# Sharing the last weight matrix 13 to 15 between the lower and upper 64 partitions, with its odd blocks on another DMA queue

## The chip, the cores and the metric

The kernel runs on one core of one Trainium2 chip. A core has a matmul engine (TensorE, PE in the profile, with its weight loads as PEld), VectorE (DVE), ScalarE (ACT), GpSimd (POOL) and SyncE (SP). Sixteen DMA engines bring data from HBM into the on-chip memory, which has 128 partitions. The metric is the device time of one execution in microseconds (us), as the median of several runs.

## The reference, cut to what matters

Two layers, each attention against a long cache followed by a gated feed-forward with ReLU, for two batch rows and one new token, all in float32:

```
x = x + attention(layernorm(x), k_cache, v_cache, wq, wo)   # D=512, 32 query heads, 8 kv heads, 32768 keys, head size 128
x = x + ffn(layernorm(x), W_gate, W_up, W_down)             # F=1792
x = x + attention(layernorm(x), k_cache, v_cache, wq, wo)   # the same caches and weights again
x = x + ffn(layernorm(x), W_gate, W_up, W_down)
# ffn(x): gate = relu(x @ W_gate); h = gate * (x @ W_up); return h @ W_down
```

The caches are 537 MB, and each layer reads them once.

## The kernel before

A class `Tape` records every operation in program order, works out from the memory regions who must wait for whom, and writes the program at the end. For that reason nearly all instructions carry one line number in the profile, L214 (the call in `emit`), and are told apart by their tiles. A DMA is recorded with a *lane*: transfers of one lane are ordered one behind the other, and a lane has a semaphore of its own. Transfers that `fetch` issues go through SP and take the lanes `lane0` to `lane15` in turn.

One large tile, `arena`, holds all data that streams through: three slots of 16384 columns at `X`, `Z` and `Y`, and behind them a ring. In attention the halves of each head's keys and values come into the slots. In layer 1 (the second one, `last` in the code) the slots are used up towards the end: the second half of the last head's keys stands in `X`, the first half of its values in `Z`, and the second half of the values comes in three pieces into `Y`.

`feed_forward(last, total)` then runs the feed-forward. Partitions carry four groups of 32: group j has the slice j of F, 448 columns or 14 blocks of 32.

- Up and gate: 32 units, of which unit e adds the product for k-tile kt into column group j of one of two PSUM banks, `acc` for the gate and `op` for up. The four j run side by side in the four 32-column groups of the PE. The weights `wgu` come in `UNITS[1] = (16, 8, 8)` units per transfer, into `X`.
- ACT applies ReLU with the layernorm's factor `rs`, which POOL computes with one power operation; DVE multiplies by the up half and transposes, in two pieces of columns, 0 to 256 and 256 to 448. The result `hT` holds 14 blocks of 32 columns.
- Down: block e of `hT` is multiplied with block e of `wd` (128 partitions by 512 columns). `spread` does this as four matmuls that write four column groups of `small[1]`. The blocks come in `DOWN[1] = (4, 4, 2, 2, 1, 1)` per transfer, into `Z`, as soon as the PE has read the values that stood there.
- `warm(n)` is a matmul whose result nobody reads; it stands between pieces of work.

In the program's text a float32 matmul is one call; in the trace it is two instructions, each with its weight load.

The order of the transfers on SP's queue at the end of layer 1 is: second half of the last keys, first half of the last values, the output weights `wo`, three pieces of values, three of `wgu`, six of `wd`. Before the end POOL has one operation left, the power for `rs`.

Of the kernel before, what the change touches and what calls it, by code (L numbers as in the profile page):

```python
# [6 lines left out]
AF = mybir.ActivationFunctionType  # L7
# [4 lines left out]
P = 128  # L12
D = 512
HKV, REP, DH, SK = 8, 4, 128, 32768
NB = 2
F = 1792
NG = HKV * NB
NT = 8
KT = D // P
FS = F // 4  # L20
NC = F // P
# [12 lines left out]
X, Z, Y, FLOW = 0, ROW, 2 * ROW, 3 * ROW  # L34
# [6 lines left out]
ARENA = OWN + 2 * D  # L41
# [7 lines left out]
XT_AT, SQ_AT = OWN + D, OWN + D + P  # L49
# [5 lines left out]
AGAIN = (KEPT, 12 * D), (12 * D, REST * D), (REST * D, 26 * D), (26 * D, ROW)  # L55

UNITS = (5, 3, 2, 1, 5, 2, 3, 4, 2, 3, 2), (16, 8, 8)
DOWN = (4, 3, 2, 4, 1), (4, 4, 2, 2, 1, 1)
QUERY = 4, 2, 3, 3, 1, 3, 2, 3, 2, 2, 3, 2, 2

C_SAME, C_SELH, C_PAIR, C_COL, C_HALF, C_MEAN, C_END = 0, 128, 144, 176, 178, 180, 181
# [13 lines left out]
def settled(a):  # L75
    return a.now if isinstance(a, Moving) else a


class Tape:
# [26 lines left out]
        return ap.tensor.name, p, p + rows, c, end  # L106

    def add(self, engine, call, args, kw):
        lane, also = kw.pop("lane", None), kw.pop("also", ())
        op = Op()  # L110
        op.engine, op.call, op.args, op.kw, op.waits = engine, call, args, kw, {}
        outs = [settled(args[0])] + [kw[k] for k in ("accum_out",) if k in kw]
        ins = [a for a in map(settled, (*args[1:], *kw.values(), *also)) if isinstance(a, bass.AP) and not any(a is o for o in outs)]
        key = lane or engine
        op.token = key, self.count.get(key, 0) + 1
        self.count[key] = op.token[1]
        needs = {}
        for ap, write in [(a, False) for a in ins] + [(a, True) for a in outs]:
            at = self.regions(ap)
            if at is None:  # L120
                continue
            name, p0, p1, c0, c1 = at
            left = []
            for was in self.seen.get(name, ()):
                q0, q1, d0, d1, wrote, other = was
                if p0 < q1 and q0 < p1 and c0 < d1 and d0 < c1 and (write or wrote):
                    if engine != "tensor" or other.token[0] != engine:
                        k, n = other.token
                        if n > needs.get(k, (0, None))[0]:
                            needs[k] = n, other  # L130
                if not (write and p0 <= q0 and q1 <= p1 and c0 <= d0 and d1 <= c1):
                    left.append(was)
            self.seen[name] = left
        for ap, write in [(a, False) for a in ins] + [(a, True) for a in outs]:
            at = self.regions(ap)
            if at is not None:
                self.seen.setdefault(at[0], []).append((*at[1:], write, op))
        if lane in self.before:
            needs.setdefault(lane, (op.token[1] - 1, self.before[lane]))
        if lane is not None:  # L140
            self.before[lane] = op
        known = self.known.setdefault(engine, {})
        loop = self.spot if engine in LOOPED else None
        lap = known if loop is None else self.lap.setdefault(engine, {})
        for k, (n, other) in needs.items():
            told = any(o.clock.get(k, 0) >= n for e, (_, o) in needs.items() if e != k)
            if lap.get(k, 0) < n and not told:
                op.waits[k] = n
        for k in op.waits:
            n, other = needs[k]  # L150
            for e, m in ((k, n), *other.clock.items()):
                known[e] = max(known.get(e, 0), m)
                lap[e] = max(lap.get(e, 0), m)
        op.clock = dict(known)
        op.spot = None
        if loop is not None:
            place = self.place.get(engine, 0)
            op.spot = (*loop, place)
            self.place[engine] = place + 1
        self.index[op.token] = len(self.ops)  # L160
        self.ops.append(op)
        return op
# [143 lines left out]
                    engine.reg_add(regs[k], regs[k], v + step[k] - held[k])  # L306


def attention_reglu_decode(nc, hold, x, k, v, wq, wo, wgu, wd, out):
    tape = Tape(nc)  # L310
    pe, dve, act, pool, sp = map(tape.engine, ("tensor", "vector", "scalar", "gpsimd", "sync"))

    def sbuf(name, width):
        return hold.enter_context(nc.sbuf_tensor(name, [P, width], F32))[:, :]
# [4 lines left out]
    arena = sbuf("arena", ARENA)  # L319
# [9 lines left out]
    def tile(at, width):  # L329
        return arena[:, at : at + width]  # L330
# [17 lines left out]
    def ring(width):  # L348
        at = turn[1] if turn[1] + width <= RING[1] else turn[3]
        turn[1] = at + width  # L350
        return at

    def fetch(at, src, lane=None, also=()):
        t = arena[:, at : at + src.shape[-1]]
        if lane is None:
            lane = f"lane{turn[2] % LANES}"
            turn[2] += 1
        sp.dma_start(t, src, lane=lane, also=also)
        return t
# [30 lines left out]
    def warm(width, bank=acc):  # L390

        pe.matmul(bank[:32, :width], pair, mean_cols.to_broadcast([P, width]), start=True, stop=True)

    def centred(total, idle=False):
        mp = small[0]
        xT, sq, ss = tile(XT_AT, P), tile(SQ_AT, KT * NB), one()
        xv = xT.rearrange("p (a b) -> p a b", b=32)
        if idle:
            warm(224)
        pe.matmul(mp[:, :NB], total[:, 0:1].to_broadcast([P, P]), col, start=True, stop=True)  # L400
        if idle:
            warm(224)
        dve.transpose(xT, xq)
        mean = bass.AP(mp.tensor, mp.offset, [mp.ap[0], [0, KT], [1, NB]])
        dve.tensor_tensor(xv[:, :, :NB], xv[:, :, :NB], mean, ALU.subtract)
        dve.tensor_tensor(sq.rearrange("p (a b) -> p a b", b=NB), xv[:, :, :NB], xv[:, :, :NB], ALU.mult)
        dve.tensor_reduce(ss, sq.rearrange("p (a b) -> p b a", b=NB), AX.X, ALU.add)
        return xv, ss
# [15 lines left out]
    def spread(tot, rows, w, start, stop):  # L424
        for c in range(4):
            pe.matmul(tot[32 * c : 32 * c + rows.shape[-1], :P], rows, w[:, c * P : (c + 1) * P], start=start, stop=stop)
# [127 lines left out]

    def feed_forward(last, total):
        xT, ss = centred(total, not last)
        gh, hT = tile(WIDE_AT, FS), tile(XT_AT, FS)
        up = acc, op
        begins = {sum(UNITS[last][:e]): n for e, n in enumerate(UNITS[last])}
        for e in range(8 * KT):  # L560
            if e in begins:
                n = begins[e]
                t, at = fetch(X + e * FS if last else ring(n * FS), wgu[:, e * FS : (e + n) * FS]), e
            s, kt, j = e // 16, e // 4 % 4, e % 4
            pe.matmul(up[s][32 * j : 32 * j + 32, :FS], xT[:, kt, :], t[:, (e - at) * FS : (e - at + 1) * FS],
                      start=kt == 0, stop=kt == KT - 1)
            if e == 3:
                rs = factor(ss, True)
            if last and e in (15, 23):
                warm(448, scores[:, 0, :])  # L570
            elif not last and e in (23, 27):
                warm(224)
            if e == 15:
                act.activation(gh, up[0][:, :FS], AF.Relu, scale=rs[:, 0:1])
        warm(448)
        for a, e in ((0, 256), (256, FS)):
            dve.scalar_tensor_tensor(gh[:, a:e], up[1][:, a:e], rs[:, 0:1], gh[:, a:e], ALU.mult, ALU.mult)
            dve.transpose(hT[:, a:e], gh[:, a:e])
        rows = hT.rearrange("p (a b) -> p a b", b=32)
        tot = small[1]  # L580
        c = 0
        for n in DOWN[last]:
            t = fetch(Z + c * D if last else ring(n * D), wd[:, c * D : (c + n) * D])
            for e in range(c, c + n):
                spread(tot, rows[:, e, :], t[:, (e - c) * D : (e - c + 1) * D], e == 0, e == NC - 1)
            c += n
            if c in ((4, 8) if last else (4, 7, 9)):
                warm(448)
            elif last and c in (10, 12):
                warm(224)  # L590
        return add(tot, last)

    total = one()
    dve.tensor_reduce(total[:, :1], xq, AX.X, ALU.add)
    for L in range(NLAYER):
        last = L == NLAYER - 1
# [4 lines left out]
        a, c, b = (X, Z, Y) if not last else (Z, X, Y)  # L601

        weights, other = [tile(WO_AT + at * WO, WO) for at in ((1, 0) if last else (0, 1))]
# [42 lines left out]
        if last:  # L646
            n, e = divmod(KEPT, D)
# [32 lines left out]
        n = seq[NG - 1]  # L680
        for lo, hi in ENDING if last else FLOWN:
            t = fetch(b + lo * D, v[n, 1, :, lo * D : hi * D])
# [44 lines left out]
```

## Time and profile before

| | |
|---|---|
| median of 3 runs | 2556.69 us (2556.3 to 2556.88) |
| the profiled execution: its own time | 2556.44 us |
| the profiled execution: span from the first to the last instruction | 2555.0 us |
| bytes moved by DMA | 1103.28 MB, mean 432 GB/s |
| busy share of the span: PE, DVE, ACT, POOL | 52%, 6%, 2%, 1% |
| mean granted clock of the PE | 0.751 |

Times inside the trace are counted from the span's start. Between the span and the execution's time lie 1.44 us. A row of the timeline gives start, length, engine, line, operation, tiles and the idle time before it with what ended it; a row of the windows gives the busy time of each engine in a stretch, the granted PE clock, the mean busy share of the 16 DMA engines, and what they moved.

### The profile page before, as it was taken

How to read it: one execution, taken by the hardware profiler on the slowest of the kernel's cores; microseconds unless marked ns; L12 is line 12 of the kernel's file. 1: busy time of each engine (PE TensorE's matmuls, PEld its weight loads, DVE VectorE, ACT ScalarE, POOL GpSimd, SP SyncE). 2: the span in 40 equal slices, each digit the busy share in tenths (PEclk: the TensorE clock that was granted, in tenths of full speed). 3: DMA queues.
4: the chain of work that ended last, by engine and by line, in shares of the span. 5: the costliest groups of instructions: out<-in, count | busy, mean ns of one | idle time of the engine just before them, and what ended most of it. 6: DMA issues, size and time to landing. Idle time of an engine off the chain costs nothing.

```text
span 2555.0 us, 20568 instructions
## 1 busy us (share of the span) xinstructions
PE 1332.5 (52%) x9542; PEld 364.7 (14%) x9542; DVE 156.9 (6%) x409; ACT 60.3 (2%) x82; POOL 18.2 (1%) x25
## 2 busy tenths in 40 slices
PE   4554545445444554455586554455445544454456
PEld 1111111111111111111121111111111111111112
DVE  1000000000000000000111000000000000000001
ACT  0000000000000000000000000000000000000000
POOL 0000000000000000000000000000000000000000
PEclk9777767777777777777798777777766777677778
DMA  9999999999999999999999999999999999999999
GB/s 425 429 440 427 428 442 430 440 429 434 434 430 440 430 433 434 430 440 430 424 422 440 431 439 429 434 434 433 437 429 435 434 433 436 429 437 432 434 435 391
DMA packets 26526, 1103.28 MB, mean 432 GB/s; under 512 B 2952, under 2 KB 3216, under 8 KB 6928
## 3 DMA queue, kind: packets, MB, share of 16 engines
q1 hardware_dynamic: 26496, 1103.06, 100.0%
q8 instruction: 12, 0.20, 0.0%
q14 instruction: 2, 0.02, 0.0%
q10 hardware_dynamic: 16, 0.00, 0.0%
HBM read 1102.99 MB, written 0.07 MB: 432 GB/s over the span
## 4 chain that ended last, share of the span: by engine, by line
DMA 73%; PE 26%; issue 0%; SPq 0%; DVE 0%; ACT 0%; ACTq 0%
DMA arena<-k 37%; DMA arena<-v 34%; PE acc L214 12%; PE pair L214 11%; DMA arena<-wd 1%; PE op L214 1%; PE small L214 1%; DMA arena<-wgu 1%; DMA arena<-wq 1%; SPq L214 0%; DVE pair L214 0%; DVE stat L214 0%; DVE arena L214 0%; DVE small L214 0%; DVE xq L214 0%
## 5 line engine op out<-in xcount | busy, mean ns | idle before, releaser
L214 PE MATMUL acc<-arena 128*16 128x512 f32 (+2 forms) x4288 | 616.3, 730 | 530.8 <-DMA arena<-v 521.5
L214 PE MATMUL pair<-arena,qz 128*32 128x512 f32 x4098 | 587.8, 727 | 558.9 <-DMA arena<-k 558.9
L214 PEld LDWEIGHTS pair<-arena,qz 128*32 128x32 f32 x4098 | 150.2, 131 | 987.1 <-issue 699.1
L214 PEld LDWEIGHTS acc<-arena 128*16 128x16 f32 (+1 forms) x4288 | 137.7, 113 | 972.5 <-issue 603.1
L214 ACT ACTIVATE arena<-pair,stat 128x1024 f32<-128x1024 f32 x32 | 35.6, 1113 | 2386.9 <-DVE stat L214 2386.9
L214 DVE TENSOR_SCALAR arena<-acc,stat 128x512 f32<-128x512 f32 (+1 forms) x39 | 25.5, 667 | 1052.1 <-PE acc L214 1052.1
L214 DVE TENSOR_REDUCE stat<-pair 128x1 f32<-128x1024 f32 x32 | 39.2, 1224 | 633.9 <-PE pair L214 633.9
L214 DVE STREAM_TRANSPOSE arena<-arena 128x512 f32<-128x512 f32 (+1 forms) x68 | 43.4, 674 | 40.8 <-ACT arena L214 40.7
L214 PE MATMUL small<-stat,cst 128*128 128x1 f32 (+1 forms) x72 | 16.2, 295 | 48.6 <-ACT arena L214 48.6
L214 PE MATMUL small<-arena,cst 128*128 128x32 f32 x64 | 13.1, 286 | 51.6 <-DVE arena L214 51.6
L214 PEld LDWEIGHTS small<-cst,arena 128*128 128x128 f32 x264 | 32.1, 191 | 28.9 <-issue 27.2
L214 PE MATMUL small<-cst,arena 128*128 128x4 f32 x264 | 35.0, 256 | 0.5 <-DVE arena L214 0.5
L214 PE MATMUL op<-arena,oT 128*2 128x512 f32 (+1 forms) x312 | 34.4, 526 | 0.4 <-DVE oT L214 0.3
L214 DVE MEMSET oT<- 128x8 f32 x33 | 2.1, 65 | 511.7 <-PE op L214 511.7
L214 POOL COPY arena<-arena 128x2048 f32<-128x2048 f32 (+1 forms) x7 | 13.4, 1921 | 2191.4 <-PE op L214 2045.7
L214 PE MATMUL op<-arena 128*32 128x448 f32 (+1 forms) x128 | 20.0, 572 | 5.6 <-DMA arena<-wq 3.1
L214 PEld LDWEIGHTS small<-stat,cst 128*128 128x128 f32 x72 | 13.2, 229 | 56.9 <-ACT arena L214 52.2
L214 PEld LDWEIGHTS small<-arena,cst 128*128 128x128 f32 x64 | 9.5, 188 | 80.5 <-DVE arena L214 80.5
L214 ACT ACT_TABLE_LOAD x16 | 20.5, 1283 | 11.4 <-DMA xq<-x 11.2
L214 PE MATMUL acc<-cst 128*32 128x448 f32 (+1 forms) x48 | 18.3, 479 | 0.0
L214 PE MATMUL small<-cst,stat 128*128 128x2 f32 x8 | 1.7, 287 | 18.7 <-DVE stat L214 18.1
L214 PE MATMUL small<-arena 128*32 128x128 f32 x224 | 8.8, 277 | 3.0 <-DMA arena<-wd 2.3
(63 smaller groups left out, 98.8 us busy)
## 6 DMA issues: line engine op xcount, KB each, us to landing
arena<-wo SPq DMA_DIRECT2D x6, 2048.0 KB, 32.0
arena<-v SPq DMA_DIRECT2D x2, 4096.0 KB, 37.8
arena<-wo SPq DMA_DIRECT2D x4, 1024.0 KB, 26.0
arena<-wd SPq DMA_DIRECT2D x4, 1024.0 KB, 23.4
arena<-wq SPq DMA_DIRECT2D x5, 768.0 KB, 6.3
arena<-wgu SPq DMA_DIRECT2D x1, 3584.0 KB, 44.1
arena<-wgu SPq DMA_DIRECT2D x2, 1792.0 KB, 48.4
arena<-v SPq DMA_DIRECT2D x2, 1536.0 KB, 40.9
```

The costliest lines, as they stand in the source:

```text
L214: ins = getattr(engine, op.call)(*args, **op.kw)
```

## The change

Only the feed-forward of layer 1 changes. Its F = 1792 columns are no longer cut into four slices of 448 but into 416, 416, 480 and 480 (`WIDTHS`), so the lower 64 partitions (groups 0 and 1) have 13 blocks of the way down and the upper 64 have 15. Twelve blocks are common to all partitions and come through SP as before, from a new array `wdm`, in transfers of 4, 4, 2, 1 and 1 blocks. The remaining ones, one block below and three above, come into the free columns of `X` behind `wgu` (`SIDE`), through POOL's queue, from the arrays `low` and `high`. They are 16 transfers, each to eight partitions that lie four apart, of 6144 bytes per partition above and 2048 below, high and low in turn. `loose` leaves out the waits of these transfers for each other. The bytes that are moved stay the same: 64 x 13 + 64 x 15 blocks are 128 x 14.

```
-DOWN = (4, 3, 2, 4, 1), (4, 4, 2, 2, 1, 1)
+DOWN = (4, 3, 2, 4, 1), (4, 4, 2, 1, 1)
+SHARED = sum(DOWN[1])
+BLOCKS = 13, 13, 15, 15
+SIDE = X + 2 * KT * F
+WIDTHS = (FS,) * 4, tuple(32 * n for n in BLOCKS)
...
-                    if engine != "tensor" or other.token[0] != engine:
+                    if (engine != "tensor" or other.token[0] != engine) and not (loose and other.token[0] == lane):
...
-        if lane in self.before:
+        if lane in self.before and not loose:
...
+        if last:
+            for at in (r + t for r in (0, 32) for t in range(4)):
+                for p, src in ((P // 2, high), (0, low)):
+                    n = src.shape[-1]
+                    rows = bass.AP(arena.tensor, arena.offset + (p + at) * ARENA + SIDE, [[4 * ARENA, 8], [1, n]])
+                    pool.dma_start(rows, src[at // 32, at % 32], lane="side", loose=True)
...
-            pe.matmul(up[s][32 * j : 32 * j + 32, :FS], xT[:, kt, :], t[:, (e - at) * FS : (e - at + 1) * FS],
+            pe.matmul(up[s][32 * j : 32 * j + 32, : widths[j]], xT[:, kt, :], t[:, place(e) - lo : place(e + 1) - lo],
...
-        for a, e in ((0, 256), (256, FS)):
+        for a, e in ((0, 256), (256, wide)):
...
+        if last:
+            for e in range(SHARED, max(BLOCKS)):
+                p = 0 if e < min(BLOCKS) else P // 2
+                spread(tot, rows[p:, e, :], tile(SIDE + (e - SHARED) * D, D)[p:], e == SHARED, False)
...
-            elif last and c in (10, 12):
+            elif last and c == 10:
                 warm(224)
```

The PE's program from the end of the up product on, before the change (a `warm` is `acc<-cst`, the matmuls of the way down are `small<-arena`):

```order
L214 MATMUL acc<-cst 32x448 [waits scalar_done]
L214 MATMUL small<-arena 32x128 [waits vector_done,lane13_done]
L214 MATMUL small<-arena 32x128 x15
L214 MATMUL acc<-cst 32x448
L214 MATMUL small<-arena 32x128 [waits lane14_done]
L214 MATMUL small<-arena 32x128 x15
L214 MATMUL acc<-cst 32x448
L214 MATMUL small<-arena 32x128 [waits vector_done,lane15_done]
L214 MATMUL small<-arena 32x128 x7
L214 MATMUL acc<-cst 32x224
```

The same place of the PE's program with the change (`side_done` counts the landings of POOL's transfers):

```order
L218 MATMUL acc<-cst 32x448 [waits scalar_done]
L218 MATMUL small<-arena 32x128 [waits vector_done,side_done]
L218 MATMUL small<-arena 32x128 x11
L218 MATMUL small<-arena 32x128 [waits lane13_done]
L218 MATMUL small<-arena 32x128 x15
L218 MATMUL acc<-cst 32x448
L218 MATMUL small<-arena 32x128 [waits lane14_done]
L218 MATMUL small<-arena 32x128 x15
L218 MATMUL acc<-cst 32x448
L218 MATMUL small<-arena 32x128 [waits lane15_done]
L218 MATMUL small<-arena 32x128 x7
L218 MATMUL acc<-cst 32x224
```

Twelve matmuls on the odd blocks 12, 13 and 14 stand ahead of the common ones, and DVE's second wait has moved from block 8 to the first matmul of the way down.

POOL's program at the end, with the change (before it, the power stood right behind the copies):

```order
L218 COPY arena<-arena 128x2048 [waits tensor_done] x3
L218 DMA arena<-high 8x1536 [waits tensor_done]
L218 DMA arena<-low 8x512
L218 DMA arena<-high 8x1536
L218 DMA arena<-low 8x512
L218 DMA arena<-high 8x1536
L218 DMA arena<-low 8x512
L218 DMA arena<-high 8x1536
L218 DMA arena<-low 8x512
```

Four more such pairs follow, and then the power, which now stands behind sixteen DMAs.

More of the change, by code (lines that the diff above doesn't have):

```diff
@@ L108, in add @@
     def add(self, engine, call, args, kw):
-        lane, also = kw.pop("lane", None), kw.pop("also", ())
+        lane, also, loose = kw.pop("lane", None), kw.pop("also", ()), kw.pop("loose", False)
         op = Op()
@@ L306, in loop, with attention_reglu_decode @@
                     engine.reg_add(regs[k], regs[k], v + step[k] - held[k])
-def attention_reglu_decode(nc, hold, x, k, v, wq, wo, wgu, wd, out):
+def attention_reglu_decode(nc, hold, x, k, v, wq, wo, wgu, wd, wdm, low, high, out):
     tape = Tape(nc)
@@ L556, in feed_forward, with place @@
         xT, ss = centred(total, not last)
-        gh, hT = tile(WIDE_AT, FS), tile(XT_AT, FS)
+        widths = WIDTHS[last]
+        wide = max(widths)
+        gh, hT = tile(WIDE_AT, wide), tile(XT_AT, wide)
         up = acc, op
+        def place(e):
+            return e // 4 * F + sum(widths[: e % 4])
+        if last:
[4 more added lines that the diff above has]
+                    pool.dma_start(rows, src[at // 32, at % 32], lane="side", loose=True)
         begins = {sum(UNITS[last][:e]): n for e, n in enumerate(UNITS[last])}
@@ L562, in feed_forward @@
                 n = begins[e]
-                t, at = fetch(X + e * FS if last else ring(n * FS), wgu[:, e * FS : (e + n) * FS]), e
+                lo, hi = place(e), place(e + n)
+                t = fetch(X + lo if last else ring(hi - lo), wgu[:, lo:hi])
             s, kt, j = e // 16, e // 4 % 4, e % 4
-            pe.matmul(up[s][32 * j : 32 * j + 32, :FS], xT[:, kt, :], t[:, (e - at) * FS : (e - at + 1) * FS],
+            pe.matmul(up[s][32 * j : 32 * j + 32, : widths[j]], xT[:, kt, :], t[:, place(e) - lo : place(e + 1) - lo],
                       start=kt == 0, stop=kt == KT - 1)
@@ L573, in feed_forward @@
             if e == 15:
-                act.activation(gh, up[0][:, :FS], AF.Relu, scale=rs[:, 0:1])
+                act.activation(gh, up[0][:, :wide], AF.Relu, scale=rs[:, 0:1])
         warm(448)
-        for a, e in ((0, 256), (256, FS)):
+        for a, e in ((0, 256), (256, wide)):
             dve.scalar_tensor_tensor(gh[:, a:e], up[1][:, a:e], rs[:, 0:1], gh[:, a:e], ALU.mult, ALU.mult)
@@ L580, in feed_forward @@
         tot = small[1]
+        if last:
+            for e in range(SHARED, max(BLOCKS)):
+                p = 0 if e < min(BLOCKS) else P // 2
+                spread(tot, rows[p:, e, :], tile(SIDE + (e - SHARED) * D, D)[p:], e == SHARED, False)
         c = 0
         for n in DOWN[last]:
-            t = fetch(Z + c * D if last else ring(n * D), wd[:, c * D : (c + n) * D])
+            t = fetch(Z + c * D if last else ring(n * D), (wdm if last else wd)[:, c * D : (c + n) * D])
             for e in range(c, c + n):
-                spread(tot, rows[:, e, :], t[:, (e - c) * D : (e - c + 1) * D], e == 0, e == NC - 1)
+                spread(tot, rows[:, e, :], t[:, (e - c) * D : (e - c + 1) * D], not last and e == 0, e == (SHARED if last else NC) - 1)
             c += n
@@ L719 @@
     }
+    at = np.cumsum((0, *WIDTHS[1]))
+    down = [a["B_W_down"][lo:hi].reshape(-1, 32, D) for lo, hi in zip(at, at[1:])]
+    arrays["wdm"] = con(np.stack([d[:SHARED] for d in down]).transpose(0, 2, 1, 3)).reshape(P, SHARED * D)
+    for name, two in (("low", down[:2]), ("high", down[2:])):
+        side = np.stack([d[SHARED:] for d in two])
+        arrays[name] = con(side.reshape(2, -1, 8, 4, D).transpose(0, 3, 2, 1, 4)).reshape(2, 4, 8, -1)
     nc = bacc.Bacc("TRN2", target_bir_lowering=False, num_devices=1, dynamic_dma_scratch_size=256)
```

## The prediction

> **What bounds the kernel now.** I read the page first, then the chain that ended last, then the last 60 us in the timeline and by windows, since all that the change touches happens there. From the page:
>
> ```profile
> GB/s 425 429 440 427 428 442 430 440 429 434 434 430 440 430 433 434 430 440 430 424 422 440 431 439 429 434 434 433 437 429 435 434 433 436 429 437 432 434 435 391
> HBM read 1102.99 MB, written 0.07 MB: 432 GB/s over the span
> DMA 73%; PE 26%; issue 0%; SPq 0%; DVE 0%; ACT 0%; ACTq 0%
> ```
>
> The transfers run at one rate from start to end; only the last of the 40 slices is lower. So the kernel is bound by its 1103 MB, and a change in its tail can only move what lies around the arrival of the last bytes. The chain that ended last says so too:
>
> ```profile
> 2521.66 30.85 DMA arena<-wd
> 2552.52 0.04 issue
> 2552.56 0.47 PE small L214 x8
> 2553.05 0.29 DVE xq L214
> ```
>
> The end waits for the last piece of `wd`. But how much spare time does the PE have beside that stream? That decides here, and it stands in the timeline (start, length, engine, idle time before it):
>
> ```profile
> 2543.79 0.18 PEld L214 LDWEIGHTS op<-arena 128*32 128x32 f32 x7 [0.20 <-issue]
> 2545.73 0.92 PE L214 MATMUL acc<-cst 128*32 128x448 f32 x2
> 2546.06 0.48 DVE L214 SCALAR_TENSOR_TENSOR arena<-op,stat,arena 128x256 f32<-128x256 f32 x1 [8.28 <-PE op L214]
> 2546.58 0.45 DVE L214 STREAM_TRANSPOSE arena<-arena 128x256 f32<-128x256 f32 x1
> 2546.95 0.38 DVE L214 SCALAR_TENSOR_TENSOR arena<-op,stat,arena 128x192 f32<-128x192 f32 x1
> 2547.14 0.84 PEld L214 LDWEIGHTS small<-arena 128*32 128x32 f32 x32 [1.30 <-DMA arena<-wd]
> 2547.18 1.08 PE L214 MATMUL small<-arena 128*32 128x128 f32 x32 [0.53 <-DVE arena L214]
> 2547.36 0.38 DVE L214 STREAM_TRANSPOSE arena<-arena 128x192 f32<-128x192 f32 x1
> 2548.75 0.82 PEld L214 LDWEIGHTS small<-arena 128*32 128x32 f32 x32 [0.59 <-DMA arena<-wd]
> 2549.57 0.22 PEld L214 LDWEIGHTS acc<-cst 128*32 128x32 f32 x2
> 2550.43 0.33 PEld L214 LDWEIGHTS small<-arena 128*32 128x32 f32 x9 [0.24 <-issue]
> 2551.28 0.38 PEld L214 LDWEIGHTS small<-arena 128*32 128x32 f32 x16 [0.30 <-DMA arena<-wd]
> 2552.56 0.16 PEld L214 LDWEIGHTS small<-arena 128*32 128x32 f32 x8 [0.32 <-DMA arena<-wd]
> ```
>
> The last `wgu` has come by 2543.79; the PE finishes up, DVE multiplies and transposes, and the way down starts at 2547.14, on DVE's first transpose (2546.58 + 0.45 = 2547.03). Its last weight load ends at 2552.72, so it lasts 5.58 us. Of these, 112 weight loads cost 0.84 / 32 = 0.0262 us each, 2.94 together. A `warm(448)` costs what passes from 2549.57 to 2550.76 less the 16 loads in between: 1.19 - 0.42 = 0.77; there are two, and two `warm(224)` at half of that: 2.31. The rest, 5.58 - 2.94 - 2.31 = 0.33 us, is all that the PE really waits for `wd`. The way down is bound by the stream and by the PE almost equally. Whatever delays its start by more than 0.33 us moves the end.
>
> **The change part by part.** Where POOL's transfers start and what they meet:
>
> ```profile
> 2493.82 0.60 PE L214 MATMUL pair<-arena,qz 128*32 128x512 f32 x4
> 2537.86 0.55 POOL L214 TENSOR_TENSOR stat<-stat,cst 128x1 f32<-128x1 f32 x1 [217.00 <-DVE stat L214]
> 2541.53 0.63 ACT L214 ACTIVATE arena<-acc,stat 128x448 f32<-128x448 f32 x1 [43.60 <-PE acc L214]
> 2494.50:2543.70 49.20, 31.60 (x237) 9.81 (x238) 6.48 (x22) 1.84 (x3) 0.55 (x1) 0.79 0.99 422
> ```
>
> POOL waits for the last matmul on the keys in `X`, which ends at 2494.4. The DMA engines are 0.99 busy from then to the last `wgu`, so POOL's bytes find no free place and push SP's back.
>
> 1. *The stream.* 512 KB (524,288 bytes) now go ahead of the last `wgu` instead of behind it: 0.524 MB / 432 GB/s = 1.21 us. Values and `wgu` arrive that much later, and `wd`, two blocks shorter, ends where it did. The delay of the values is harmless, since the PE waits for `wgu` behind them anyway. That of the last `wgu` is on the path: +1.21. Bounds: 0 if the bytes fit into what is left of the engines' time, and 1.82 if the high rows load only half of the engines: 64 rows of 6144 bytes are 393,216, on eight engines at 432 / 16 = 27 GB/s each. I take the middle, an even spread.
> 2. *Wider up product.* The four groups run side by side, so 480 columns count instead of 448. The last eight units are two such rounds, each as long as one `warm(448)`, about 1.5 us together (their loads start at 2543.79 and the warm behind them runs at 2545.73); 32/448 of it is +0.11.
> 3. *DVE.* Its second pieces go from 192 to 224 columns: by the rows (0.48 - 0.38) / 64 and (0.45 - 0.38) / 64 us per column, 32 columns are +0.05 and +0.035, together +0.09.
> 4. *The odd blocks stand first.* Blocks 12 to 14 are columns 384 to 480 of `hT`, made by DVE's second transpose. The first matmul of the way down used to wait for the first transpose (end 2547.03) and now waits for the second (end 2547.36 + 0.38 = 2547.74): +0.71. Everything on the PE is queued behind it, the 12 common blocks too, whose data have long been there.
> 5. *The way down itself.* 15 blocks of odd and common data are 120 loads, 3.15 us; two `warm(448)` 1.54; one `warm(224)` 0.38: 5.07 against 5.58 before, because the second `warm(224)` is gone and the waits for `wd` too, which now always comes first: -0.51.
> 6. *POOL's queue.* Sixteen issues stand ahead of the power. It could end as late as about 2546 before DVE would notice (ACT's 0.63 and the multiplication at 2547.3 behind it); from 2494.4 that is some 3.2 us per transfer. I cost it at nothing; what it costs without that cover is a rival.
>
> Sum: 1.21 + 0.11 + 0.09 + 0.71 - 0.51 = +1.61 us. With term 1 at its bounds it is +0.40 and +2.22. The stream's end is no limit any more: the last `wd` still lands near 2552.5, and the PE's last load ends near 2554.3. Made against the profiled execution (2556.44) this gives 2558.05; the median of the runs lies 0.25 above that execution, so I predict 2558.3. That is 0.06% slower. Less than about 0.2% (5.1 us) either way is what a measurement of this kernel can hardly tell from no change, so the forecast is "within 0.2%".
>
> **The rivals.**
>
> *A. One half of the engines carries the high rows.* The engines do not end together. The windows' last two columns, DMA share and GB/s:
>
> ```profile
> 2549.75:2550.00 0.25, 0.25 (x5) 0.03 (x1) 0.00 (x0) 0.00 (x0) 0.00 (x0) 1.00 0.84 320
> 2550.75:2551.00 0.25, 0.25 (x7) 0.22 (x3) 0.00 (x0) 0.00 (x0) 0.00 (x0) 1.00 0.32 123
> 2551.75:2552.00 0.25, 0.25 (x13) 0.17 (x8) 0.00 (x0) 0.00 (x0) 0.00 (x0) 1.00 0.17 66
> ```
>
> From a share of 0.84 it takes two more microseconds to zero: a third of the engines is about 1 us behind the rest. A landing counts when the last engine is done. If the high rows fall on eight engines and those include late ones, term 1 is 1.82 and the time 2558.9; if the late ones are all in the other half, which gets a quarter of the bytes, it is 0.61 and the time 2557.7. The rows don't tell which engine is late, so this is a spread around the forecast. The Trainium skill, "DMA: Bandwidth & Descriptors", section "Why a DMA increments its semaphore by 16 and not by 1", has such a rule: a transfer of eight rows uses eight engines, and on GpSimd's path these are consecutive ones from a cursor that goes round; with high and low in turn, that would put all high rows on one half. No row here shows GpSimd's transfers.
>
> *B. The bytes are hidden, and it does not get slower.* The window from 2494.50 shows 422 GB/s, and the best slices of the page 440. A second queue could give the engines a packet where SP's alone leaves a gap. The window moved 422 x 49.2 = 20.76 MB; with 0.524 more at 440 it takes 48.4 us, term 1 becomes -0.8 and the time 2556.3. It decides at about 436 GB/s, where term 1 is -0.40 and the sum zero. Against it: the share of 0.99 leaves half a microsecond at most, and the new packets are smaller, not larger, than those they run beside.
>
> *C. The PE's clock falls in the way down.* The PE now stands idle from the end of its warm, 1.2 us later than before, to DVE's second transpose. The granted clock is the third column from the end:
>
> ```profile
> 2530.40:2533.70 3.30, 1.83 (x38) 1.37 (x37) 1.26 (x7) 0.00 (x0) 0.00 (x0) 1.00 0.92 395
> 2533.90:2537.10 3.20, 1.95 (x10) 0.50 (x10) 0.00 (x0) 0.00 (x0) 0.00 (x0) 0.50 0.98 417
> 2544.10:2547.40 3.30, 2.77 (x28) 0.86 (x24) 1.27 (x4) 0.00 (x0) 0.00 (x0) 1.00 0.99 411
> 2547.50:2550.80 3.30, 3.30 (x80) 2.21 (x73) 0.24 (x1) 0.00 (x0) 0.00 (x0) 1.00 0.91 353
> ```
>
> A window with 1.83 us of PE work was followed by half clock, one with 2.77 was not. In the fourth window the PE will be idle for about 1.3 us and busy for 2.0: between the two, nearer to the one that fell. Against it: the work is denser there than in the first row, two-column matmuls for the most part. At half clock the 3.4 us of PE work left at 2550.9 double: 2561.7. The Trainium skill, "TensorE: Matmul & The Clock Gate", section "Part 1: The HAM clock gate (the "warmup" mystery)", has the clock fall after at least one idle window of about 3.4 us; by that an idle 1.3 us does nothing. The trace disagrees: 1.83 us of work in the window was not enough.
>
> *D. POOL's transfers come one by one.* The only small transfers on another queue beside SP's stream are the two of `x`, at the start:
>
> ```profile
> L214 ACTq DMA_DIRECT2D xq<-x x2: 513/800/1088, 1.1 to 10.5; - x2
> L214 DVE TENSOR_REDUCE stat<-xq x1: 285/285/285, 17.8 to 17.8; 128x1 f32<-128x128 f32 x1
> ```
>
> The second went out at 10.5 when the first had landed, and the reader started at 17.8: 9.4 and 7.3 us for 2 KB each. Sixteen of 7.3 us in a row would end at 2494.4 + 117 = 2611, and the kernel would take some 2615. It decides at about 3.3 us per transfer, where POOL's power or the landing would hold up the way down at 2549. Against it: no wait is between the sixteen, so they are in flight together; and the packets beside them get smaller from 2504.8 on (`x` ran beside rows of 64 KB). That the skill puts a fixed 2 us on each small transfer ("DMA: Bandwidth & Descriptors", section "Anatomy of one DMA — SWDGE (gpsimd) path") would even in a row be 32 us and hidden.
>
> **How the numbers follow.** Chances: the forecast with an even spread 0.53 (2557.5 to 2559.1), A 0.20 (2557.7 or 2558.9, inside or near that), B 0.13 (2555.9 to 2556.9), C 0.09 (2560.5 to 2562.3), D 0.05 (above 2562). The range 2556.1 to 2560.0 keeps the forecast, A and most of B, and leaves out C, D and the far end of B, less than 2 in 10; the likeliest case alone is 2557.1 to 2559.3. Faster than 2551.6 no case reaches: 0.01. Above 2561.8 lie D and a third of C: 0.07. The rest is 0.92.
>
> **What would show it.** Term 1: the last `wgu` in the chain or the waits about 1.2 us later (PE's third group of `op<-arena` near 2545.0), the values too. Terms 3 and 4: the first `small<-arena` load directly behind DVE's second transpose, near 2549.2. Term 5: no wait of the PE for `wd` behind that, and a chain that ended last which goes through PE and DVE back to `wgu`, with `wd` no longer in it. Term 6: POOL's issues done long before its power at about 2539. Rival A shows in the DMA share of the last windows, B as a last `wgu` at 2543.8 or earlier, C as a granted clock of 0.5 after 2550.9, D as a wait for `low` or `high`. The prediction is wrong if the way down starts within 0.3 us of 2547.14, or if a transfer of POOL's ends behind 2549.

## The result and the profile after

The changed kernel takes 2562.38 us in the median of 13 runs (2560.74 to 2563.99), against 2556.52 for the kernel before in as many. The ratio is 1.0022, 95% interval 1.0015 to 1.003: slower by 5.9 us. The forecast was 2558.3, in a range that ended at 2560.0. The profiled execution took 2562.38 us with a span of 2561.0.

From the page of the changed kernel; q0 is POOL's queue:

```profile
GB/s 424 428 439 429 438 430 439 429 439 429 438 429 438 428 433 435 431 437 429 428 431 432 435 433 434 433 433 433 434 433 432 435 433 434 433 434 434 434 433 348
q0 software_dynamic: 512, 0.53, 0.1%
HBM read 1102.99 MB, written 0.07 MB: 431 GB/s over the span
```

The bytes are the same, and the loss lies in the last of the 40 slices, 348 GB/s instead of 391; the mean of the other 39 is 433 before and after. The chain that ended last, in order of time:

```profile
2491.32 49.62 DMA arena<-wgu
...
2549.13 0.39 another core or an unknown queue
...
2549.56 1.84 PE op L218 x16
...
2551.51 0.49 DVE arena L218
...
2552.84 0.42 DVE arena L218
...
2553.39 2.01 PE small L218 x56
...
2558.58 0.50 PE small L218 x8
2559.10 0.29 DVE xq L218
```

`wd` is gone from it. The end now goes back through the way down and DVE's second transpose to `wgu`, as the prediction said (the 0.39 us that the chain calls unknown are, in the timeline below, the PE's wait for the last `wgu`). But this last `wgu`, for which the PE waited until 2549.56, was expected near 2545.0. The timeline has the places that the prediction's terms speak of:

```profile
2549.56 1.82 PE L218 MATMUL op<-arena 128*32 128x416 f32 x16 [0.43 <-DMA arena<-wgu]
2551.51 0.48 DVE L218 SCALAR_TENSOR_TENSOR arena<-op,stat,arena 128x256 f32<-128x256 f32 x1 [7.79 <-PE op L218]
2552.84 0.41 DVE L218 STREAM_TRANSPOSE arena<-arena 128x224 f32<-128x224 f32 x1
2553.36 0.19 PEld L218 LDWEIGHTS small<-arena 128*32 128x32 f32 x8 [2.27 <-issue]
2558.04 0.71 PEld L218 LDWEIGHTS small<-arena 128*32 128x32 f32 x16
```

Where the time went stands in one row of the windows, for the 35 us in which POOL issues fourteen of its sixteen transfers. Before and after (the last two columns are DMA share and GB/s):

```profile
2495.00:2530.00 35.00, 20.81 (x145) 5.40 (x146) 4.04 (x11) 1.20 (x2) 0.00 (x0) 0.80 0.98 422
```

```profile
2495.00:2530.00 35.00, 17.72 (x118) 4.74 (x122) 3.58 (x8) 1.21 (x2) 7.36 (x14) 0.76 0.99 384
```

The DMA engines are as busy as before and move 9% less: 38 GB/s over 35 us are 1.33 MB, 3.1 us of the stream. Something makes packets longer while the odd blocks come in. The packet records of the trace say the same: from 2507 to 2530 a 32 KB row of values took 1.213 us in the median before the change, and up to 1.69 us beside POOL's rows. The experiments ask what does it: POOL's way of issuing, the number of transfers, the bytes on a second queue, or the place where the rows go.

### The profile page after: what moved, and what is told of

Read it like the earlier page. It is cut to its first block, busy times and chain, and to the rows that moved or that the text cites. A ratio compares the mean times of both kernels' runs of the same rounds, so it can differ in the third digit from the quotient of the medians.

```text
span 2561.0 us, 20594 instructions
## 1 busy us (share of the span) xinstructions
PE 1340.5 (52%) x9548; PEld 367.7 (14%) x9548; DVE 157.0 (6%) x409; ACT 60.4 (2%) x82; POOL 26.6 (1%) x41
## 4 chain that ended last, share of the span: by engine, by line
DMA 73%; PE 26%; issue 0%; DVE 0%; SPq 0%; another core or an unknown queue 0%; ACT 0%; ACTq 0%; DVEq 0%
DMA arena<-k 37%; DMA arena<-v 33%; PE acc L218 12%; PE pair L218 11%; DMA arena<-wgu 2%; PE small L218 2%; PE op L218 1%; DMA arena<-wq 1%; DMA arena<-wd 0%; SPq L218 0%; DVE arena L218 0%; DVE stat L218 0%; DVE xq L218 0%; ACT arena L218 0%
## 5 line engine op out<-in xcount | busy, mean ns | idle before, releaser
L218 PE MATMUL pair<-arena,qz 128*32 128x512 f32 x4098 | 594.5, 734 | 554.8 <-DMA arena<-k 554.7
L218 PE MATMUL op<-arena 128*32 128x512 f32 (+3 forms) x128 | 19.6, 572 | 5.8 <-DMA arena<-wgu 2.9
L218 PE MATMUL small<-arena 128*32 128x128 f32 (+1 forms) x232 | 9.0, 277 | 3.9 <-DMA arena<-wd 2.4
```

The costliest lines, as they stand in the source:

```text
L218: ins = getattr(engine, op.call)(*args, **op.kw)
```

## The experiments

Each was timed beside the kernel before on the same chip, which took 2556.66 to 2556.71 us there. Most intervals reach 0.09% to either side, 2.3 us, so a difference smaller than that is read from medians and traces and isn't clear of noise by itself.

**Sixteen transfers made two.** Edit, with arrays laid out to match:

```
-            for at in (r + t for r in (0, 32) for t in range(4)):
-                for p, src in ((P // 2, high), (0, low)):
-                    ...
-                    pool.dma_start(rows, src[at // 32, at % 32], lane="side", loose=True)
+            for p, src in ((P // 2, high), (0, low)):
+                n = src.shape[-1]
+                pool.dma_start(arena[p : p + P // 2, SIDE : SIDE + n], src, lane="side", loose=True)
```

> The odd blocks' bytes stay on POOL's queue, but in 2 transfers of 64 rows instead of 16 of eight. Known: with 16 transfers the last wgu landed 5.8 us later than before the change (2543.7 to 2549.5), of which the bytes explain 1.2. Theory 1 (each transfer on POOL's queue costs, by its 16 completions and the packets around them): 4.6 us / 16 = 0.29 us each, two cost 0.6, the last wgu lands 1.8 us later than before the change and the kernel takes about 2558.5. Theory 2 (the bytes on a second queue cost, however they are cut): unchanged, last wgu 5.8 later, about 2562.4. Theory 3 (the bytes fall on half of the engines, since eight rows use eight engines): 64 rows use all sixteen, last wgu 1.2 to 2 later, 2558 to 2558.7.

Measured 2562.07 us (ratio 1.0021, 1.0012 to 1.003). Neither the count of transfers nor the choice of eight rows is what costs here; theories 1 and 3 are wrong in this form. The time is the one of theory 2.

**The same two transfers on SP's queue, behind `wgu`.** The two calls become `sp.dma_start` and stand behind the loop over the units.

> The same two transfers of 64 rows on SP's own queue, behind wgu and ahead of wd, so there is no second queue and nothing ahead of wgu. All theories of the queue expect the last wgu where it was before the change (about 2543.7). What is left are the terms 2 to 5 of the prediction: up product wider, DVE wider, way down behind the second transpose, shorter way down: +0.40 us, so 2556.9 (bytes of the odd blocks now land between wgu and wd, about 1.2 us behind the last wgu, before the way down starts). If the split 13 to 15 itself were the cost, it would stay near 2562.

Measured 2562.04 us (ratio 1.0021, 1.0012 to 1.0031). That was not expected by any theory of the queue: without a second queue, and with nothing ahead of `wgu`, it is just as slow. The windows show where, before and then in this run:

```profile
2540.00:2545.00 5.00, 5.00 (x47) 1.63 (x40) 0.00 (x0) 0.63 (x1) 0.00 (x0) 0.94 0.99 412
2545.00:2550.00 5.00, 4.47 (x78) 2.36 (x71) 1.61 (x4) 0.00 (x0) 0.00 (x0) 1.00 0.99 399
```

```profile
2540.00:2545.00 5.00, 3.64 (x32) 1.13 (x22) 0.00 (x0) 0.66 (x1) 0.00 (x0) 1.00 1.00 240
2545.00:2550.00 5.00, 3.40 (x18) 1.23 (x18) 0.00 (x0) 0.00 (x0) 0.00 (x0) 0.66 1.00 302
```

The engines are fully busy at 240 and 302 GB/s while the odd blocks come in, instead of 412 and 399. A row of 6144 bytes took 0.45 us there in the median of its packet records, and 0.234 where it ran fast. The rows of the lower half were slow as well: 2048 bytes took 0.158 us in the median, where the change's own took 0.09. The `wgu` packets beside them took about twice their time, which delays the last `wgu` to 2546.6 although it stands ahead in the queue. Beside this longer wait the PE's mean granted clock is lower too (0.66 in the second row), so this run's end mixes both.

**Sixteen tiny transfers.** Each row of the sixteen brings 16 of its columns; the rest of the odd blocks is not loaded.

```
-                    rows = bass.AP(arena.tensor, arena.offset + (p + at) * ARENA + SIDE, [[4 * ARENA, 8], [1, n]])
+                    rows = bass.AP(arena.tensor, arena.offset + (p + at) * ARENA + SIDE, [[4 * ARENA, 8], [1, 16]])
-                    pool.dma_start(rows, src[at // 32, at % 32], lane="side", loose=True)
+                    pool.dma_start(rows, src[at // 32, at % 32, :, :16], lane="side", loose=True)
```

> All sixteen transfers of eight rows on POOL's queue stay, but each row brings 64 bytes instead of 6144 or 2048; the rest of the odd blocks is not loaded. Theory 1 (cost per transfer): 4.6 of the 5.8 us stay, last wgu lands 4.6 us later than before the change, about 2561.2. Theory 2 (cost by bytes on a second queue) and theory 3 (bytes on half of the engines): last wgu back near 2543.7 to 2544, 2556.9 to 2557.2.

Measured 2557.19 us (ratio 1.0002, 0.9993 to 1.0011), and 418 GB/s in the window from 2495 to 2530. Sixteen issues on POOL and their completions cost nothing that shows; theory 1 falls. With the split 13 to 15, the wider products and the wait on the second transpose this run is 0.5 us above the kernel before, inside its interval; terms 2 to 5 say 0.40.

**The sixteen transfers on ACT's queue.** `pool.dma_start` becomes `act.dma_start`.

> The sixteen transfers of eight rows, same bytes, on ACT's queue instead of POOL's. If any second queue beside SP's costs this (theory 2 or 3 without regard to the queue), it stays near 2562. If it is POOL's way of making transfers (theory 1 tied to POOL: descriptors in memory and sixteen completions each), the last wgu lands 1.2 to 2.4 us later than before the change (2.4 if all sixteen use the same eight engines), 2558 to 2559.2.

Measured 2562.69 us (ratio 1.0023, 1.0014 to 1.0032), 378 GB/s in that window. It is not POOL. So far the bytes cost, on any queue, in any cut. What all slow runs share is that each transfer fills rows of only one half of the partitions.

**One transfer of 128 partitions on SP's queue.** The same 512 KB in the same place of the queue as in the second run; the odd blocks' places then hold other numbers.

```
+        if last:
+            sp.dma_start(arena[:, SIDE : SIDE + 2 * D], side, lane="side")
```

> As the run with the odd blocks on SP's queue behind wgu (2562.0), but the same 512 KB come as one transfer of 128 partitions by 4096 bytes instead of 64 by 6144 and 64 by 2048; the odd blocks' places then hold other numbers than they should. Theory A (a transfer into only half of the partitions makes all engines write through half of the memory's inputs, and what runs beside it slows down too): the slow stretch of 240 and 302 GB/s between 2540 and 2550 goes, and the time is the 2556.9 that the terms 2 to 5 give. Theory B (reading from the small new arrays is slow): unchanged, 2562.

Measured 2557.33 us (ratio 1.0003, 0.9994 to 1.0012). The slow stretch is gone:

```profile
2540.00:2545.00 5.00, 4.79 (x44) 1.79 (x40) 0.00 (x0) 0.66 (x1) 0.00 (x0) 1.00 1.00 411
2545.00:2550.00 5.00, 3.50 (x68) 1.79 (x60) 1.68 (x4) 0.00 (x0) 0.00 (x0) 1.00 0.97 392
```

Same bytes, a small array of its own as well, same queue: what differs is which rows a transfer fills, 128 in one instead of 64 in each of two. Theory B falls. Theory A fits, and so does a finer one (C): the half as such is not slow, but writing into it from engines that otherwise serve the other half.

**Low first.**

```
-                for p, src in ((P // 2, high), (0, low)):
+                for p, src in ((0, low), (P // 2, high)):
```

> The change with low ahead of high in each pair. Theory A (half of the partitions at a time is slow whichever engine writes): no difference, 2562.4. Theory C (eight rows go to eight engines in turn, and it is slow where engines write to the half that the other engines serve; low first swaps the halves): the packets beside POOL's keep their usual length, the last wgu comes 1.2 to 1.8 us later than before the change, and the time is 2558.2 to 2558.9.

Measured 2562.38 us (ratio 1.0022, 1.0013 to 1.0031), 391 GB/s from 2495 to 2530. The order within a pair decides nothing. This is against theory C as long as one takes it that POOL's transfers go to the two halves of the engines in turn.

**All rows into the lower half, and all into the upper half, on ACT's queue.** A pair of runs that differ in one number, the first partition; sixteen transfers of eight rows by 4096 bytes, the odd blocks' places hold other numbers.

```
+            for e in range(16):
+                at = 0 + e // 8 * 32 + e // 2 % 4          # 64 + ... in the twin
+                rows = bass.AP(arena.tensor, arena.offset + at * ARENA + SIDE + (1 - e % 2) * 2 * D, [[4 * ARENA, 8], [1, 2 * D]])
+                act.dma_start(rows, side[8 * e : 8 * e + 8], lane="side", loose=True)
```

> Sixteen transfers of eight rows by 4096 bytes on ACT's queue, all into the lower 64 partitions; the odd blocks' places hold other numbers than they should. Same bytes, queue and count as its twin into the upper 64. Theory C, if ACT's eight rows always use the engines that serve the lower half: usual packet lengths, but these eight engines carry all 512 KB, so the last wgu comes 2.4 us later than before the change: 2559.4. Theory A: as slow as the twin, about 2562.5.

> The twin: the same sixteen transfers on ACT's queue, all into the upper 64 partitions. Theory C: the same eight engines write into the other half, packets of SP's beside them become longer, and the last wgu comes 6 us later or more: 2563. Theory A: the same as into the lower half. Theory B: both the same too.

Measured 2559.51 us for the lower half (ratio 1.0011, 1.0002 to 1.002) and 2564.16 for the upper (1.0029, 1.0019 to 1.004). The window of the lower, then of the upper:

```profile
2495.00:2530.00 35.00, 19.43 (x130) 4.95 (x130) 3.77 (x8) 1.20 (x2) 0.00 (x0) 0.73 0.98 419
```

```profile
2495.00:2530.00 35.00, 18.04 (x114) 4.60 (x110) 3.77 (x8) 1.21 (x2) 0.00 (x0) 0.76 0.98 362
```

Same queue, count, rows and bytes: into the lower half the stream keeps its rate, into the upper half it loses 14%. That tells A from C, and A falls: half of the partitions is not slow in itself. In the upper run 488 of the 533 rows of SP's in this window took over 6% longer than rows of their size before, in the lower run one of 620. Half of SP's rows go to the lower half, so these got longer as well, beside transfers into the upper.

The lower run still ends 2.8 us later than the kernel before. If eight engines carry all 512 KB, 65,536 bytes each at 432 / 16 = 27 GB/s, that is 2.4 us. The last `wgu` comes at 2546.6 instead of 2543.8:

```profile
2546.62 1.82 PE L218 MATMUL op<-arena 128*32 128x416 f32 x16 [0.34 <-DMA arena<-wgu]
```

Of these 2.8 us, 0.4 were there before ACT's transfers began: the PE got the last keys at 2485.78 instead of 2485.36. The other 2.4 are what eight engines give. In the upper run the last `wgu` is 7.2 us late by the same count (2551.05, keys at 2485.43): the lost 60 GB/s over 35 us are 4.9 us of the stream, and with the 2.4 that makes 7.3.

**One transfer of 128 partitions on POOL's queue, ahead of `wgu`.**

```
+            pool.dma_start(arena[:, SIDE : SIDE + 2 * D], side, lane="side")
```

The odd blocks' places again hold other numbers, in this run and the two that follow.

> The 512 KB of odd blocks on POOL's queue ahead of wgu, but as one transfer of 128 partitions by 4096 bytes; the odd blocks' places then hold other numbers than they should. If the queue is harmless and only the place of the rows was dear (theory C), this is the case that the prediction took for term 1: an even spread, last wgu 1.2 us later than before the change, 2558.2. If POOL's queue itself costs, the last wgu comes later than that, up to 5.8 us and 2562.4.

Measured 2558.31 us (ratio 1.0007, 0.9998 to 1.0016); the prediction gave 2558.3 for the even spread:

```profile
2495.00:2530.00 35.00, 18.76 (x138) 4.87 (x138) 3.77 (x8) 1.21 (x2) 0.73 (x1) 0.82 1.00 426
```

POOL's queue and the place ahead of `wgu` cost what term 1 said. The last `wgu` comes at 2546.07, 2.28 us later than before; 1.05 of these were there before POOL's transfer (last keys at 2486.41 instead of 2485.36), and 1.23 remain, against 1.21 predicted.

**Eight rows into the lower half, on POOL's queue.** The lower run above with `pool` for `act`.

> The run with sixteen transfers of eight rows into the lower 64 partitions, on POOL's queue instead of ACT's (2559.5 there). If eight rows from POOL always use the same eight engines, those that serve the lower half, as ACT's do: the same, 2559.5, packets of SP's beside them at their usual length. If POOL's transfers go round over both halves of the engines: every second one writes from the other half, packets get longer (32 KB at 1.4 us instead of 1.21), and the time is 2560.5 to 2562.5.

Measured 2559.25 us (ratio 1.001, 1.0001 to 1.0019):

```profile
2495.00:2530.00 35.00, 19.76 (x146) 5.06 (x142) 3.77 (x8) 1.21 (x2) 8.39 (x16) 0.80 0.99 422
```

No loss of rate, the time of ACT's twin. So transfers of eight rows on POOL's queue behave like those on ACT's: all sixteen as if carried by engines that serve the lower half. That would also explain the run with low first: there was nothing to swap. The trace names no engine, so this is concluded from times and rates.

**Odd blocks multiplied last**, on the kernel with one POOL transfer of 128 partitions: the loop over the odd blocks moves behind the common ones, with its `start` and `stop`.

> As the run with one POOL transfer of 128 partitions, with the odd blocks multiplied behind the common ones, so that the way down starts on DVE's first transpose again. Term 4 says 0.71 us earlier start and end: 2557.5 if that run gives 2558.2. If the way down were bound by wd's landing instead, no difference.

Measured 2557.66 us (ratio 1.0004, 0.9995 to 1.0013), 0.65 less than its twin (a difference inside the intervals); term 4 said 0.71. The first `small<-arena` of the chain now stands behind one piece of DVE's work:

```profile
2548.29 0.46 DVE arena L218
2548.75 0.14 issue
2548.89 1.08 PE small L218 x32
```

None of these versions beats the kernel before, which has the odd bytes in transfers of 128 partitions behind `wgu`.

## Why the prediction was wrong, by its own steps

*Term 1 failed, in size: +1.21 predicted, +5.8 measured* (last `wgu` at 2549.5 instead of 2543.7), against bounds of 0 and 1.82. Two things make it up.

- The transfers of eight rows bring down the rate of the whole stream: 422 to 384 GB/s for 35 us, 3.1 us. The cost comes when rows of the upper half are written in these transfers: lower half alone 419 and 422, upper alone 362, the change with three quarters of its bytes in the upper half 384.
- All 512 KB come, as the lower runs' times have it, through eight engines, not through sixteen or through each eight in turn: 2.4 us for the latest engine instead of 1.2.

Together 5.5 of the 5.8; the same two give 2.4 and 7.3 for the lower and the upper run, where 2.4 and 7.2 were measured. The step of the prediction that failed is the division in term 1, 0.524 MB by 432 GB/s: it takes it that POOL's rows cost the stream their bytes at the common rate. No row of before shows otherwise, since there every large transfer fills all 128 partitions; the upper bound of 1.82 took over that common rate and was no bound. The only transfers with few rows in that trace, those of `x`, were used for the waiting time alone.

*Rival A* had half of it right: eight engines carry these rows, as far as times tell, and the latest engine counts. It gave them the high rows alone, at full rate, so 1.82. The rule named there, consecutive engines from a cursor that goes round (the Trainium skill, "DMA: Bandwidth & Descriptors", section "Why a DMA increments its semaphore by 16 and not by 1"), is not what these runs show: with it, low first or sixteen transfers into the lower half would have behaved otherwise. The same page of the Trainium skill, section "The descriptor swizzle", has each engine of a 128-partition transfer write partitions of its own, half of the engines for each half of the partitions. Why writing across the halves is slow, no run shows. That two writers share one way into the memory fits that section and the doubled row times (0.45 against 0.234 us) of the run with 64 rows in a transfer. It doesn't explain why nearly all of SP's rows got longer in the upper run, those into the lower half too. Nor did any run send eight upper rows through other engines; that the crossing is slow, and not such transfers into the upper half as such, rests on the slow lower rows of the run with 64 rows (0.158 against 0.09 us).

*Terms 3 and 4 held, 2 and 5 did not.* The first load of the way down follows DVE's second transpose (2552.84 + 0.41, load at 2553.36). From DVE's first operation to the transpose that is waited for it is 1.74 us instead of 0.97: +0.77 for terms 3 and 4, predicted 0.80. The way down lasts 5.39 us, from 2553.36 to 2558.75, against 5.58: -0.19 where term 5 said -0.51, with no wait for `wd`. The price per load was too low at one place: the first 56 loads take 1.75 us (2553.36 to 2555.11) instead of 1.47, with two gaps of 0.20 at the change to weights of 64 rows and back. Term 2 gave +0.11; from the start of the last units to DVE's first operation it took 2.27 us before (2543.79 to 2546.06) and 1.95 after (2549.56 to 2551.51), so -0.32, since the PE now waits for the last `wgu` with its earlier work done. The two misses nearly cancel. With the bytes spread evenly the time was 2558.31 against the 2558.3 predicted: term 1 was right there in its mechanism, and the close hit of the whole sum is in part luck.

*Term 6 held* in its cost, with other waits than assumed. POOL's issues and its power:

```profile
2495.05 0.72 POOL L218 DMA_DIRECT2D arena<-high  x1 [173.90 <-PE pair L218]
...
2511.61 0.52 POOL L218 DMA_DIRECT2D arena<-low  x1 [12.78 <-issue]
...
2530.03 0.52 POOL L218 DMA_DIRECT2D arena<-high  x1 [14.85 <-issue]
2530.54 0.52 POOL L218 DMA_DIRECT2D arena<-low  x1
2543.81 0.57 POOL L218 TENSOR_TENSOR stat<-stat,cst 128x1 f32<-128x1 f32 x1 [12.74 <-DVE stat L218]
```

An issue takes 0.52 us, but after seven POOL stands still for 12.8 and then 14.9 us. So the sixteen were not all in flight together, as the prediction took it against rival D. The last issue ends at 2531.1, 12.7 us ahead of the power. *Rival D* did not come true, and *B* was refuted in its sign: a second queue brought no rate. *Rival C* did not either: the windows after have a clock of 1.00 from 2545 on.

```profile
2545.00:2550.00 5.00, 4.57 (x42) 1.70 (x38) 0.00 (x0) 0.66 (x1) 0.00 (x0) 1.00 0.99 410
2550.00:2555.00 5.00, 3.50 (x66) 1.81 (x62) 1.67 (x4) 0.00 (x0) 0.00 (x0) 1.00 0.70 280
```

## What to carry to other kernels

In a kernel that lives from a full DMA stream, the cost of a transfer is not its bytes over the common rate: look which rows it fills. Transfers over all 128 partitions kept the rate on SP's and on POOL's queue (411 and 426 GB/s); 64 rows at a time, or eight rows in the upper half, slowed down what ran beside them (240 and 362). When DMA share is near 1.00 and GB/s falls, packets have become longer, and the transfers that run in that window are the place to look. And where a step's price rests on a rate that the trace shows for one shape only, the bound has to allow for another rate.

## What the runs showed of the hardware

- 64 rows in one transfer on the queue of the stream: 240 GB/s with a DMA share of 1.00, where 128 rows of the same bytes keep 411.
- Eight rows into the lower half 419 to 422 GB/s, into the upper half 362, same queue and bytes.
- POOL's and ACT's transfers of eight rows cost the same: 2559.25 and 2559.51 us into the lower half, 2562.38 and 2562.69 for the change's own rows.
- Sixteen transfers of eight rows by 64 bytes on a second queue cost nothing that shows: 2557.19 us, 418 GB/s.
- Beside the transfers of eight rows into the upper half 488 of 533 rows of SP's got longer, beside those into the lower half one of 620.
- POOL issues seven such transfers and then stands still, 12.8 and 14.9 us in the change, 10.5 and 13.7 in the lower run. The kernel sets `dynamic_dma_scratch_size=256`; whether that sets the number was not tried.
